# Attention with a relative bias and a mixture of adapters on one core: an earlier fetch of the last tokens, five staging buffers with a lead one pair longer, and edge factors ahead of gating on GpSimd

## The chip, the core and the metric

The kernel runs on one core of a Trainium2 chip. The core has TensorE (PE in the profile, its weight loads PEld), VectorE (DVE), ScalarE (ACT), GpSimd (POOL) and SyncE (SP), each with an instruction queue of its own that it works off in order. In this kernel nearly all DMAs are issued by SyncE. The metric is the time of one execution on the device, in microseconds.

## What is computed

```python
def _attn_ref(q, k, v, bias_table):             # q, k, v: (8, 8, 576, 64)
    scores = scale * np.matmul(q, k.transpose(0, 1, 3, 2))
    ...
    bias = bias_table[bucket]                   # bucket depends on |i - j| alone
    scores = scores + bias.transpose(2, 0, 1)[None, :, :, :]
    ...
    attn = np.exp(scores)
    attn = attn / (np.sum(attn, axis=-1, keepdims=True) + 1e-09)
    return np.matmul(attn, v).astype(np.float32)

def _moe_ref(x, w_gate, A, B):                  # x: (4608, 512), 8 experts, rank 16, two per token
    logits = x @ w_gate
    ...
            z = x[mask] @ A[e]
            delta[mask] += w[mask, k, None] * (z @ B[e])
    return (x + delta).astype(np.float32)
```

The output of the attention of all heads, side by side, is the x of the adapters. The weights w are the softmax over the two largest logits of a token.

## The kernel before

The work is cut into 32 pairs: pair u is batch b = u // 4 and the two heads 2 hp and 2 hp + 1 with hp = u % 4. The main loop (L747) runs over the pairs, and all instructions stand in an order written out by hand. The 576 tokens of a batch are 512 main tokens, in four chunks of keys, and 64 last tokens, called the tail. The tails of q, k and v are fetched once for a batch, for all its heads.

Loading: `load` (L103) issues on SyncE the main tokens of q (one DMA of 256 KB) and of k and v (two of 128 KB each) of one pair into a staging pool with four buffers for each of q, k, v (L70). `load_tail` (L118) issues three DMAs of 128 KB for a batch, for tails of q and k in one tile (qkt) and of v in another (vt), of which there are two each. Their rows in memory are 64 floats long. In pair u the loop issues q and k of pair u + 4 and v of pair u + 3 (L757 to L762), in pairs with hp = 0 ahead of them the tails of batch b + 1 (L753), in pair 2 the adapter weights (`weights_load`, L283), and in pair 1, between the two, the tails of batch 1. SyncE also issues the stores of the output (L617, L605) and, at some pairs, the DMAs that transpose x (`send_x`, L355).

Casting: GpSimd turns float32 into bfloat16. `prep(u)` (L722) casts q and k of pair u + 2 (L141) and v of pair u (L137), at the head of pair u from pair 4 on. `prep_tail` (L730) casts the tail of batch b + 1: that of q and k (qkb, L149) in the pair with hp = 1 and that of v (vb, L153) in the pair with hp = 2. The adapter weights are cast by VectorE at the end of pair 3 (`weights_cast`, L290, its first cast L291) and turned by TensorE in pairs 4 and 5 (L300).

Scores: TensorE turns q and k of pair u + 1 in pair u (L317), VectorE copies the result (qkT, L321). `keys` makes the scores of one chunk with the bias (L376, L381), `keys_exp` their exponential on ScalarE (pk, L387), four of 128x1024 a pair. `edges` (L409), at the end of pair u for pair u + 1, makes the scores between the main tokens and the tail and their exponential (pt, L424). The bias of pt is not added before the exponential but multiplied in afterwards: `edge_bias` (L426), two multiplications on GpSimd with the factors ELC and ET (L430, L432), in the pair to which pt belongs.

Values: in pair u + 1 TensorE multiplies the probabilities of pair u with v: `values_b` and `values_a`, the chunks by L440, the tail's keys by L450, which reads pt, and the tail's rows by L464. VectorE divides by the sums (L508, L521, L528) and writes x.

Adapters: x is turned by TensorE (L348) or by a transposing DMA (L357), multiplied with A and the gate weights (L541), and VectorE finds the two largest logits, their sum, the argument of the tanh and the mask (L555, L560, L562, L565). The gating itself is `moe_w` (L568): a tanh on ScalarE, whose program place is behind the second exponential of a pair, and three instructions on GpSimd (g L574, gate L576, zt L578). zt is turned by TensorE (L586) one to three pairs later, ahead of that pair's L440 of `values_b`, multiplied with B (L593), and VectorE adds x (ot, L596). On GpSimd the gating of a pair (`run(gate1...)`, L768) stands behind that pair's casts and ahead of its `edge_bias`; in the last pair alone `edge_bias` stands ahead of it (L766).

Of the kernel before, what the change touches and what calls it, by code (L numbers as in the profile page):

```python
# [26 lines left out]
def _ap(t, offset, dims):  # L27

    return bass.AP(tensor=t.tensor, offset=t.offset + offset, ap=[list(t.ap[0])] + dims)
# [8 lines left out]
def kernel(  # L38
# [12 lines left out]
    B, H, S, D = q.shape  # L51
# [5 lines left out]
    HP = H // 2  # L57
# [9 lines left out]
    ctx.enter_context(tc.manual_schedule())  # L67

    cp = ctx.enter_context(tc.tile_pool(name="const", bufs=1))
    stg = ctx.enter_context(tc.tile_pool(name="staging", bufs=4))  # L70
    stt = ctx.enter_context(tc.tile_pool(name="tailstaging", bufs=2))
    qkp = ctx.enter_context(tc.tile_pool(name="qk", bufs=2))
    ep = ctx.enter_context(tc.tile_pool(name="probs", bufs=2))
# [17 lines left out]
    NU = len(units)  # L91
# [11 lines left out]
    def load(u, names="qkv", eng=nc.sync):  # L103
        b, hp = units[u]
        for nm in names:
            src = {"q": q, "k": k, "v": v}[nm]
            t = stg.tile([128, 2, 4 * D], FP32, name=f"{nm}s", tag=f"{nm}s")
            heads = src[b, 2 * hp:2 * hp + 2, :SM, :]
            if nm != "q":
                for h in range(2):  # L110
                    eng.dma_start(out=t[:, h, :].rearrange("p (g x) -> p g x", g=2),
                                      in_=heads[h].rearrange("(g p c) d -> p g (c d)", g=2, c=2))
            else:
                eng.dma_start(out=t, in_=heads.rearrange("h (p c) d -> p h (c d)", c=4))
            stage[(u, nm)] = t


    def load_tail(b, names="qkv", g0=0, g1=HP, eng=nc.sync):  # L118
        for nm in names:
            src = {"q": q, "k": k, "v": v}[nm][b, :, SM:, :]  # L120
            if nm == "v":
                t = stt.tile([64, H, D], FP32, name="vt", tag="vt")
                eng.dma_start(out=t, in_=src.rearrange("g p d -> p g d"))
            else:
                if (b, "qk") not in tstage:
                    tstage[(b, "qk")] = stt.tile([128, H, D], FP32, name="qkt", tag="qkt")
                t = tstage[(b, "qk")]
                o = 0 if nm == "q" else 64
                eng.dma_start(out=t[o:o + 64, 2 * g0:2 * g1],
                              in_=src[2 * g0:2 * g1].rearrange("g p d -> p g d"))  # L130
            tstage[(b, nm)] = t
# [151 lines left out]
    def weights_load():  # L283
        nc.sync.dma_start(out=A4f.rearrange("p e c r -> p e (c r)"),
                          in_=moe_A.rearrange("e (p c) r -> p e (c r)", c=4))
        nc.sync.dma_start(out=G4f.rearrange("p c e -> p (c e)"),
                          in_=moe_w_gate.rearrange("(p c) e -> p (c e)", c=4))
        nc.sync.dma_start(out=Bf, in_=moe_B.rearrange("e r d -> (e r) d"))
# [97 lines left out]
    def keys_exp(u, c):  # L386
        nc.scalar.activation(probs[u][0][c], scs.pop(c), ACT.Exp, scale=scale)  # L387
# [38 lines left out]
    def edge_bias(u, eng=nc.gpsimd):  # L426
        b, hp = units[u]
        pt = probs[u][1]
        tl = _ap(pt, 64 + 256 + 96, [[SM, 2], [128, 2], [1, 32]])
        nc.gpsimd.tensor_tensor(tl, tl, _ap(ELC, hp * 64, [[SM, 2], [32, 2], [1, 32]]), op=ALU.mult)  # L430
        te = _ap(pt[64:], 64 + 128, [[SM, 2], [1, 128]])
        eng.tensor_tensor(te, te, ET[64:, :, hp, :], op=ALU.mult)  # L432
# [289 lines left out]
    def prep(u):  # L722
        b, hp = units[u]
        if u + 2 < NU:
            for nm in ("q", "k") if u > 2 else ("k",):
                cast(u + 2, nm, nc.gpsimd)
        if u:
            cast(u, "v", nc.gpsimd)
# [18 lines left out]
    for u in range(NU):  # L747
        b, hp = units[u]
        if hp == 0 and b:
            moe(b - 1, u)  # L750
        if u > 3:
            prep(u)
        if hp == 0 and 0 < b < B - 1:  # L753
            load_tail(b + 1)
        if u == 2:
            weights_load()
        if u + 4 < NU:  # L757
            load(u + 4, "qk")
        if u == 1:
            load_tail(1)  # L760
        if u + 3 < NU:
            load(u + 3, "v")  # L762
        for c in KO[:2]:
            keys(u, c)
            keys_exp(u, c)
        if u == NU - 1:  # L766
            edge_bias(u)
        run(gate1.pop(u, []))  # L768
        if u:
            if u < NU - 1:  # L770
                edge_bias(u)
            if u < 4:
                prep(u)
            if u == 6:
                nc.gpsimd.tensor_scalar(Bc, Bf, 0.5, None, op0=ALU.mult)
            prep_tail(u)
        zb, ta, xa = zs.pop(u, []), zts.pop(u, []), xas.pop(u, [])
        if u:
            pa = pva.pop(u - 2, None)
            oa = 256 if xa or hp == 0 else (ER + E) * (len(zb) > 1)  # L780
            ia = (XO - oa) // 64

            def bank_b():
                pv = values_b(u - 1)
                zl = pv[:, 260:260 + ER + E]
                for gr, t in zb[:1]:
                    moe_z(gr, t, zl, False)
                o = 260 + (ER + E) * bool(zb)
                for i, (gr, t) in enumerate(ta[ia:]):
                    moe_t(gr, t, pv, o + i * 64)  # L790
                return pv, zl

            if pa is not None:
                for gr, t in xa:
                    turn_x(gr, t, pa)
                values_x(u - 2, pa)
                for i, (gr, t) in enumerate(ta[:ia]):
                    moe_t(gr, t, pa, oa + 64 * i)
                za = pa[:, :ER + E]
                for gr, t in zb[1:]:  # L800
                    moe_z(gr, t, za, True)
                for gr, t in xa:
                    copy_x(gr, t)
                for gr, t in ta[:ia]:
                    moe_tc(gr, t)
                normalise_x(u - 2, pa)
                for gr, t in zb[1:]:
                    moe_zc(gr, t, za)
            pv, zl = bank_b()
            for gr, t in ta[ia:]:  # L810
                moe_tc(gr, t)
            normalise_b(u - 1)
            for gr, t in zb[:1]:
                moe_zc(gr, t, zl)
            if u < 16:
                run(dl2.pop(u, []))
            if hp == 0:
                corners(pa[:, :256], b)
            run(send.pop(u, []))
        else:  # L820
            t = Turn()
            turn_tail(t, 0, 2)
            copy_tail(t, 0, 2)
            corners(mp.tile([128, 256], FP32, name="cps", tag="mm"), 0)
        keys(u, KO[2])
        keys_exp(u, KO[2])
        run(dl2.pop(u, []))
        if 0 < u < NU - 1:
            t = Turn()
            turn_qk(t, u + 1)  # L830
            if hp == HP - 1:
                turn_tail(t, b + 1)
            xt = xts.pop(u, [])
            x0 = 16 - 4 * len(xt)
            for i, (gr, c) in enumerate(xt):
                for j in range(4):
                    t.block(x0 + 4 * i + j, gr.x[c][:, j * 128:j * 128 + 128])
            copy_qk(t, u + 1)
            if xt:
                gr, c = xt[0]  # L840
                gr.open()
                t.copy(gr.xT[:, c:c + len(xt)], x0, 4 * len(xt))
            if hp == HP - 1:
                copy_tail(t, b + 1)
        keys(u, KO[3])
        keys_exp(u, KO[3])
        run(dls.pop(u, []))
        if u in (4, 5):
            weights_turn(u - 4)
        if u == 0:  # L850
            factors_l()
            factors_t()
            corners_bias(0)
            edge_bias(0)
            prep(0)
        else:
            if hp == 0:
                corners_bias(b)
            values_a(u - 1)
            if u == NU - 1:  # L860
                values_x(u - 1, pva[u - 1])
            normalise_a(u - 1)
            if u == NU - 1:
                normalise_x(u - 1, pva[u - 1])
            for gr, i in zb:
                at(gates, gr.late or u, moe_g, gr, i)
            run(gates.pop(u, []))
            run(sendx.pop(u, []))
        if u < 3:
            cast(u + 2, "q", nc.vector)  # L870
        if u == 3:
            weights_cast()
        if u == NU - 1:
            break
        if u:
            open_probs(u + 1)
            edges(u + 1)


        order = slots[-3:]  # L880
# [242 lines left out]
```

## Time and profile before

| | |
|---|---|
| median of three runs | 196.53 us (194.33, 196.53, 196.64) |
| the profiled execution | 195.78 us, its span 193.9 us |
| granted TensorE clock | 0.992 of full speed |
| VectorE, GpSimd busy | 136.2 us (70%), 138.7 us (72%) |
| moved by DMA | 41.77 MB, 215 GB/s in the mean |

The times of engines and instructions come from the one profiled execution, counted from the start of its span. A row of a timeline gives start, duration, engine, line of the kernel, operation and tiles, and in brackets how long the engine had been idle before it and what released it. A wait for several events is put down to the one that came last by the profile, which can be the wrong one. A row of the stretches gives, for a piece of the span, the busy time of PE, PEld, DVE, ACT and POOL with the number of instructions, the granted clock, the share of DMA and its GB/s.

### The profile page before, as it was taken

To read this page: it belongs to the slowest core of one execution; us is meant where nothing else is said; L and a number is where in the kernel's file an instruction comes from. 1 tells how busy PE (TensorE), PEld (TensorE's weight loads), DVE (VectorE), ACT (ScalarE), POOL (GpSimd) and SP (SyncE) were. 2 spreads that over 40 slices of the span, in tenths; PEclk is the share of its full clock that TensorE was granted. 3 is DMA by queue.
4 is the path that set the end of the run, shared out by engine and by line. 5 is a ranking of instruction groups with operands and counts; after the bars stand their busy time and mean duration, and the time that the engine had idled before them with its cause. 6 is when DMAs were issued, how large, how long until landed. Compare 5 with 4: busy or idle time off the path is not lost.

```text
span 193.9 us, 11323 instructions
## 1 busy us (share of the span) xinstructions
PE 167.9 (87%) x4833; PEld 121.3 (63%) x4834; DVE 136.2 (70%) x460; ACT 166.2 (86%) x206; POOL 138.7 (72%) x286
## 2 busy tenths in 40 slices
PE   0459798999999998999989999995899999999970
PEld 0335466777777776677766676673667676666840
DVE  4421466656758975899779778984779998888760
ACT  3159999999999999999989899995898899789680
POOL 5086945898996998589978857649898885876030
PEclk9999999999999999999999999999999999999996
DMA  5679797998868996889786887689879998855356
GB/s 149 183 163 253 234 239 193 269 225 216 246 177 219 173 273 213 215 211 261 247 218 175 215 247 181 180 255 237 247 222 256 238 185 254 269 187 146 112 229 205
DMA packets 72047, 41.77 MB, mean 215 GB/s; under 512 B 25773, under 2 KB 67253, under 8 KB 71997
## 3 DMA queue, kind: packets, MB, share of 16 engines
q1 hardware_dynamic: 71084, 40.58, 77.4%
q8 instruction: 37, 0.61, 1.5%
q10 hardware_dynamic: 912, 0.48, 1.0%
q14 instruction: 14, 0.11, 0.2%
HBM read 29.67 MB, written 9.47 MB: 202 GB/s over the span
## 4 chain that ended last, share of the span: by engine, by line
PE 53%; DVE 13%; DMA 9%; ACT 9%; POOL 5%; issue 5%; SPq 3%; ACTq 1%; POOLq 0%; DVEq 0%
PE sc L376 11%; PE pv L440 11%; ACT pk L387 7%; PE sc L381 6%; DMA qkt<-in_k_dram 5%; PE tp L317 4%; PE dl L593 4%; PE pv L464 4%; PE pv L450 3%; PE sc L417 3%; PE pv L541 3%; DMA Wt<-g_d 2%; DVE ot L596 2%; PE pv L348 2%; DMA ks<-in_k_dram 2%
## 5 line engine op out<-in xcount | busy, mean ns | idle before, releaser
L387 ACT ACTIVATE pk<-sc 128x1024 bf16<-128x1024 f32 x128 | 124.3, 1032 | 6.8 <-PE sc L381 6.4
L376 PE MATMUL sc<-qkT 64*64 64x512 bf16 x512 | 53.1, 394 | 2.4 <-issue 1.1
L381 PE MATMUL sc<-Wt,antw 64*64 64x384 bf16 (+1 forms) x512 | 44.5, 301 | 1.3 <-DMA Wt<-g_d 1.2
L440 PEld LDWEIGHTS <-pk 128*128 128x128 bf16 x1024 | 39.5, 98 | 7.8 <-issue 4.7
L440 PE MATMUL pv<-v,pk 128*128 128x65 bf16 x992 | 42.1, 194 | 1.7 <-POOL v L137 1.4
L424 ACT ACTIVATE pt<-sc 128x1024 bf16<-128x1024 f32 x32 | 32.8, 1025 | 10.1 <-PE sc L422 8.6
L321 DVE COPY qkT<-tp 128x1024 bf16<-128x1024 bf16 x32 | 22.1, 689 | 8.8 <-PE tp L317 7.7
L508 DVE TENSOR_TENSOR xn<-pv,rc 128x256 bf16<-128x256 f32 x56 | 23.8, 425 | 1.9
L141 POOL CAST kn<-ks 128x512 bf16<-128x512 f32 x30 | 18.4, 613 | 8.8 <-DMA ks<-in_k_dram 4.4
L376 PEld LDWEIGHTS <-qkT 64*64 64x64 bf16 x512 | 18.0, 107 | 9.7 <-issue 3.7
L432 POOL TENSOR_TENSOR pt<-pt,ET 64x256 bf16<-64x256 bf16 x32 | 21.4, 668 | 2.5
L141 POOL CAST qn<-qs 128x512 bf16<-128x512 f32 x27 | 16.5, 610 | 5.4 <-PE tp L317 3.5
L137 POOL CAST v<-vs 128x512 bf16<-128x512 f32 x32 | 20.0, 625 | 0.1
L381 PEld LDWEIGHTS <-antw 64*64 64x64 bf16 x512 | 17.9, 108 | 3.1 <-issue 2.6
L450 PE MATMUL pv<-vb,pt 128*128 128x130 bf16 x124 | 17.3, 220 | 2.4 <-POOL pt L430 2.4
L596 DVE TENSOR_TENSOR ot<-dl,xn 128x512 f32<-128x512 f32 x25 | 17.1, 685 | 0.4 <-PE dl L593 0.2
L317 PE MATMUL tp<-ident,qn 64*64 64x64 bf16 x512 | 11.7, 196 | 5.2 <-ACT qn L141 5.2
L317 PEld LDWEIGHTS <-qn 64*64 64x64 bf16 x512 | 10.7, 111 | 8.6 <-ACT qn L141 5.2
L430 POOL TENSOR_TENSOR pt<-pt,ELC 128x128 bf16<-128x128 bf16 x32 | 13.6, 426 | 1.1 <-ACT pt L424 0.6
L317 PE MATMUL tp<-ident,kn 64*64 64x64 bf16 x512 | 12.0, 197 | 2.0 <-issue 1.5
L464 PEld LDWEIGHTS <-pt 128*128 128x128 bf16 x256 | 10.5, 98 | 5.0 <-issue 5.0
L464 PE MATMUL pv<-v,pt 128*128 128x65 bf16 x248 | 13.2, 194 | 0.1
(144 smaller groups left out, 309.5 us busy)
## 6 DMA issues: line engine op xcount, KB each, us to landing
qs<-in_q_dram SPq DMA_DIRECT2D x32, 256.0 KB, 3.6
vs<-in_v_dram SPq DMA_DIRECT2D x64, 128.0 KB, 4.2
ks<-in_k_dram SPq DMA_DIRECT2D x62, 128.0 KB, 4.0
out_dram<-ot SPq DMA_DIRECT2D x25, 256.0 KB, 3.8
vt<-in_v_dram SPq DMA_DIRECT2D x8, 128.0 KB, 5.6
out_dram<-fot SPq DMA_DIRECT2D x4, 256.0 KB, 2.1
qkt<-in_q_dram SPq DMA_DIRECT2D x7, 128.0 KB, 5.6
qkt<-in_k_dram SPq DMA_DIRECT2D x7, 128.0 KB, 4.0
```

Source lines behind the costliest of these rows:

```text
L141: copy(t.rearrange("p c h d -> p h c d"), s)
L317: nc.tensor.transpose(self.ps[h * 64:h * 64 + 64, f, x * 64:x * 64 + 64], src[rows, h * 64:h * 64 + 64], ident[rows, rows])
L321: nc.vector.tensor_copy(_ap(dst, 0, [[64, 2], [128, n], [1, 64]]), self.ps[:, :, x * 64:(x + n) * 64].rearrange("p f (x t) -> p f x t", t=64))
L376: nc.tensor.matmul(sc[prt, h, :], lhsT=kT[rows, c * 128 + f * 64:c * 128 + f * 64 + 64], rhs=qT[rows, :], start=True, stop=False, skip_gro ...
L381: nc.tensor.matmul(_ap(sc[prt, h, :], p0, [[128, 4], [1, n]]), lhsT=turned_w(h), rhs=_ap(Wt[rows, hp, :], (1 - e) * GY + y0, [[GY, 4], [1, ...
L387: nc.scalar.activation(probs[u][0][c], scs.pop(c), ACT.Exp, scale=scale)
L424: nc.scalar.activation(probs[u][1][:, 64:], sc.rearrange("p h x -> p (h x)"), ACT.Exp, scale=scale)
L432: eng.tensor_tensor(te, te, ET[64:, :, hp, :], op=ALU.mult)
L440: nc.tensor.matmul(pv[:, o + h * W1:o + (h + 1) * W1], lhsT=pk[c][:, h, t * 128:(t + 1) * 128], rhs=vm[:, c, h, :], start=(first and h == ...
L450: nc.tensor.matmul(_ap(pv, o + h * W1, [[130, n], [1, W1]]), lhsT=pt[:, x0:x0 + 128], rhs=tvs[b % 2][:, t // 2:t // 2 + n, 2 * hp + h, :], ...
L464: nc.tensor.matmul(pv[:, o + h * W1:o + (h + 1) * W1], lhsT=src[:, x0:x0 + 128], rhs=rhs, start=(first and h == 0), stop=False, skip_group ...
L508: nc.vector.tensor_tensor(dst, _ap(pv, 0, [[2 * W1, 2], [W1, 2], [1, D]]), _ap(rc, i, [[2, 2], [1, 2], [0, D]]), op=ALU.mult)
```

## The change

Four things change in the text; no instruction is added or removed, only their order and the number of staging buffers.

- The staging pool has five buffers instead of four for each of q, k and v.
- The tails of batch b + 2 are issued in the pair of batch b with hp = 2, for batches 2 to 7, instead of those of batch b + 1 in the pair with hp = 0. Their casts stay where they are: a tail's q and k are now issued three pairs ahead of their cast, and v four, instead of one and two. The tails of batch 1 are issued in pair 1 as before.
- Up to pair 8, q and k are issued four pairs ahead and v three; from pair 8 on five and four, so that pair 8 issues two pairs of each.
- `edge_bias` stands ahead of the gating in every pair from pair 1 on, not in the last alone.

```diff
-    stg = ctx.enter_context(tc.tile_pool(name="staging", bufs=4))
+    stg = ctx.enter_context(tc.tile_pool(name="staging", bufs=5))
...
-        if hp == 0 and 0 < b < B - 1:
-            load_tail(b + 1)
+        if hp == HP - 2 and 1 < b + 2 < B:
+            load_tail(b + 2)
         if u == 2:
             weights_load()
-        if u + 4 < NU:
-            load(u + 4, "qk")
+        for n in (u + 4,) * (u < 9) + (u + 5,) * (u > 7):
+            if n < NU:
+                load(n, "qk")
         if u == 1:
             load_tail(1)
-        if u + 3 < NU:
-            load(u + 3, "v")
+        for n in (u + 3,) * (u < 9) + (u + 4,) * (u > 7):
+            if n < NU:
+                load(n, "v")
         for c in KO[:2]:
             keys(u, c)
             keys_exp(u, c)
-        if u == NU - 1:
+        if u:
             edge_bias(u)
         run(gate1.pop(u, []))
         if u:
-            if u < NU - 1:
-                edge_bias(u)
             if u < 4:
                 prep(u)
```

## The prediction

> **What bounds the kernel now.** I read the page first, then the busy time by stretches, the waits, and the timelines of the single engines around the places that the waits point to.
>
> ```profile
> PE 167.9 (87%) x4833; PEld 121.3 (63%) x4834; DVE 136.2 (70%) x460; ACT 166.2 (86%) x206; POOL 138.7 (72%) x286
> ```
>
> and by stretches:
>
> ```profile
> 45.00:98.00 53.00, 51.54 (x1571) 38.42 (x1571) 41.30 (x137) 51.62 (x62) 44.94 (x84) 1.00 0.84 223
> 130.00:141.00 11.00, 8.05 (x249) 5.99 (x245) 6.48 (x26) 8.06 (x12) 8.92 (x19) 1.00 0.92 246
> 98.00:176.00 78.00, 72.92 (x2137) 51.99 (x2122) 64.47 (x225) 69.64 (x86) 59.52 (x118) 1.00 0.83 222
> ```
>
> TensorE and ScalarE are busy 87% and 86% of the span, so the body can only be as short as the exponentials and the products, and what can be won is idle time of ScalarE. The stretches (busy time of PE, PEld, DVE, ACT, POOL in this order) say where it lies. From 45 to 98 us ScalarE idles 53.00 - 51.62 = 1.38 us, 2.6%. From 98 to 176 us it idles 78.00 - 69.64 = 8.36 us; at 2.6% it would be 2.03, so 6.33 us are in excess there, and 2.94 of the 8.36 lie in the 11 us from 130 on. That is the place to read.
>
> ```profile
> 122.44 0.69 SPq L129 DMA_DIRECT2D qkt<-in_q_dram  x1
> ...
> 125.45 0.63 SPq L114 DMA_DIRECT2D qs<-in_q_dram  x1
> 126.12 0.98 SPq L111 DMA_DIRECT2D ks<-in_k_dram  x2
> ```
>
> then GpSimd:
>
> ```profile
> 127.32 0.61 POOL L149 CAST qkb<-qkt 128x512 bf16<-128x512 f32 x1 [0.42 <-DMA qkt<-in_k_dram]
> 128.60 0.61 POOL L141 CAST qn<-qs 128x512 bf16<-128x512 f32 x1 [0.67 <-DMA qs<-in_q_dram]
> 130.89 0.61 POOL L141 CAST kn<-ks 128x512 bf16<-128x512 f32 x1 [1.68 <-PE pv L586]
> 131.45 0.62 POOL L137 CAST v<-vs 128x512 bf16<-128x512 f32 x1
> ...
> 132.63 0.62 POOL L578 TENSOR_TENSOR zt<-z,gate 128x256 bf16<-128x256 f32 x1
> 133.20 0.42 POOL L430 TENSOR_TENSOR pt<-pt,ELC 128x128 bf16<-128x128 bf16 x1
> ```
>
> then TensorE and ScalarE:
>
> ```profile
> 132.12 0.68 PE L440 MATMUL pv<-v,pk 128*128 128x65 bf16 x16 [1.35 <-POOL v L137]
> 133.68 0.29 PE L450 MATMUL pv<-vb,pt 128*128 128x130 bf16 x2 [0.89 <-POOL pt L430]
> ```
>
> ```profile
> 134.81 1.94 ACT L387 ACTIVATE pk<-sc 128x1024 bf16<-128x1024 f32 x2 [2.39 <-PE sc L381]
> ```
>
> Each row is start, duration, engine, line, and the idle time before it. SyncE issues the tail loads of the next batch at the head of pair 20 (122.44 to 125.45: 3.01 us), and only then q and k of pair 24, whose k is issued at 126.12. GpSimd casts exactly these in its pair 21 and 22: the tail after 0.42 us of idleness, q after 0.67, k after 1.68. The profile names L586 as the releaser of the last, but the k cast reads nothing that L586 makes and the k load went out only 4.77 us before it; I take it for the load. Behind it in GpSimd's queue stand the cast of v, the gating (zt) and only then the edge factor (pt); TensorE waits 1.35 us for v and 0.89 for pt, and ScalarE 2.39 for TensorE.
>
> **Part one: the longer lead.** From pair 8 on, q, k, v are issued one pair sooner, and the tails from the pair with hp = 2, ahead of where they were by two pairs. Buffers do not object: with five of them the load of pair n takes the buffer of pair n - 5, whose cast of q and k stands two pairs ahead of that issue, the same distance as with four buffers and the shorter lead. So the waits of GpSimd on loads go, from its pair 11 on, the first whose q and k went out early.
>
> ```profile
> POOL qkb L149 <- DMA qkt<-in_k_dram: 9.4, 4, 3.5
> POOL g L574 <- ACT th L572: 6.2, 6, 2.2
> ```
>
> ```profile
> 170.10 1.02 ACT L424 ACTIVATE pt<-sc 128x1024 bf16<-128x1024 f32 x1 [0.64 <-POOL g L574]
> ```
>
> Most of GpSimd's waiting is covered: it costs only where TensorE comes to wait for GpSimd. Of the 9.4 us on tails, all but the 0.42 above fall before 31 us in GpSimd's timeline, on the loads of batches 0 and 1, which the change leaves where they are: no gain. What I book is the stretch from 130 to 141: its idle time falls from 2.94 to the 2.6% of the quiet stretch, 0.29: minus 2.65 us. To it I add the one wait of ScalarE that is put down to GpSimd, minus 0.64. Gain 3.3 us; its bounds are 0 (VectorE is as late right behind) and the 6.33 us of the excess.
>
> The five extra issues at pair 8 (q, two of k, two of v, about 2.4 us at 0.49 each by the 126.12 row) delay on SyncE the two transposes of that pair, which are read two and three pairs later. I book nothing; uncovered it would be 2.4 us once.
>
> **Part two: what the moved tail pushes back.** The tails of batch 2 used to be issued at the head of pair 4; now they are issued at the head of pair 2, in front of the adapter weights and of q, k of pair 6.
>
> ```profile
> 28.79 1.56 SPq L284 DMA_DIRECT2D A4f<-in_moe_A_dram  x1
> ```
>
> ```profile
> 37.36 0.61 SPq L129 DMA_DIRECT2D qkt<-in_q_dram  x1
> ...
> 40.06 0.57 SPq L114 DMA_DIRECT2D qs<-in_q_dram  x1
> ```
>
> and of the DMA issues (KB, us to landing), VectorE, GpSimd and TensorE:
>
> ```profile
> A4f<-in_moe_A_dram SPq DMA_DIRECT2D x1, 256.0 KB, 4.1
> ```
>
> ```profile
> 33.59 0.56 DVE L291 CAST A<-A4f 128x512 bf16<-128x512 f32 x1
> ...
> 35.51 0.18 DVE L528 RECIPROCAL rc<-pv 128x4 f32<-128x4 f32 x1 [0.41 <-PE pv L450]
> ...
> 36.45 0.69 DVE L321 COPY qkT<-tp 128x1024 bf16<-128x1024 bf16 x1 [0.30 <-PE tp L317]
> ```
>
> ```profile
> 37.03 0.61 POOL L141 CAST kn<-ks 128x512 bf16<-128x512 f32 x1 [0.16 <-DMA ks<-in_k_dram]
> ```
>
> ```profile
> 39.80 0.68 PE L440 MATMUL pv<-v,pk 128*128 128x65 bf16 x16
> ```
>
> The three tail issues took SyncE 40.06 - 37.36 = 2.70 us. SyncE issues one load after the other there, so A4f goes out at 28.79 + 2.70 = 31.49 and, landing 4.1 us after its issue, is there at 35.6; VectorE reaches its cast at 33.59 and now stands 2.0 us. Queued behind it are the normalisation of pair 2's tail rows, which frees the bank for TensorE, and the copy of qkT for pair 5, which the next scores read. VectorE's idle 0.41 and 0.30 absorb 0.7 of it, so qkT comes 1.3 us late. ScalarE is the bound here and does not get that back: plus 1.3 us. The bounds are 0 (a landing that owes less to SyncE than I think) and 2.7 (nothing absorbed).
>
> The Trainium skill has a rule that would make this dearer: DMA: Bandwidth & Descriptors, Specifications, says that pieces under 512 B do not move at line rate, and a tail moves in rows of 64 floats, 256 B. By that page the 384 KB of tails would weigh like twice the bytes, an estimate of 3.5 us at the 223 GB/s of the stretch from 45 on, 2.1 us late after the same 0.7 and 0.7, and a sum 0.8 us higher. No row here separates rings from SyncE's issue, so it stays at the upper edge.
>
> GpSimd's k of pair 6 moves from 37.03 to 39.7 by the same 2.70, and the cast of v behind it from 37.6 to 40.3; TensorE reads that v at 39.80, which becomes 41.1 with the 1.3 above: covered by 0.8. From pair 4 on the tail issue that stood there is gone, and SyncE is level again; at pair 6 and 8 the same exchange repeats with nothing like A4f in it, and I book zero.
>
> **Part three: edge factors ahead of gating.** No instruction is added. The edge factors no longer stand behind a gating that waits for tanh, 6.2 us of idle GpSimd time in all, which is hidden now; zero by itself, but it is why pt of 133.20 would be earlier. In exchange zt comes later by the two edge multiplications.
>
> ```profile
> L432 POOL TENSOR_TENSOR pt<-pt,ET 64x256 bf16<-64x256 bf16 x32 | 21.4, 668 | 2.5
> ...
> L430 POOL TENSOR_TENSOR pt<-pt,ELC 128x128 bf16<-128x128 bf16 x32 | 13.6, 426 | 1.1 <-ACT pt L424 0.6
> ```
>
> and where one pair's zt meets its reader, with VectorE's sum of the two top logits (ns min/median/max):
>
> ```profile
> 125.13 0.62 POOL L578 TENSOR_TENSOR zt<-z,gate 128x256 bf16<-128x256 f32 x1
> ```
>
> ```profile
> 125.81 0.23 PE L586 MATMUL pv<-ident,zt 128*128 128x128 bf16 x1
> ```
>
> ```profile
> L560 DVE TENSOR_TENSOR sn<-top x17: 159/307/641, 58.4 to 175.9; 128x2 f32<-128x2 f32 x14, 128x1 f32<-128x1 f32 x3
> ```
>
> That is 0.668 + 0.426 = 1.09 us. At pair 21 there is no room for it as things stand: zt ends at 125.75 and TensorE turns it at 125.81. With GpSimd no longer held up by loads (above) it is ahead by more than that, so zero; without that cover it costs 1.09 us in each pair whose zt is read in the next.
>
> **The sum.** The profiled execution took 195.78 us, its span 193.9 and 1.88 around it. 195.78 - 2.65 - 0.64 + 1.3 = 193.8. The median of the three runs shown is 196.53, 0.75 above the profiled one, and the lowest 194.33; I leave the sum on the profiled time.
>
> **The rivals.** *The early cost does not bite and the lead is worth more:* A4f is not on time by SyncE's issue alone, and the excess from 98 on is largely late loads. For it speak GpSimd's k and q waits in that stretch, against it that VectorE is busy 64.47 of the 78 us there. No early cost, and half of what I did not book of the excess, (6.33 - 3.29) / 2 = 1.5: 195.78 - 3.29 - 1.5 = 191.0.
>
> *VectorE takes the place of the loads:* GpSimd without its waits runs against VectorE's gating more often. The sum of the two top logits (sn) took from 159 to 641 ns, median 307, for two elements a partition; if all seventeen took the longest, that is 17 x 0.334 = 5.7 us more on VectorE, enough to eat the 3.3. Left is the early cost: 195.78 + 1.3 = 197.1. The Trainium skill has the rule for this spread (SBUF — State Buffer, Who interferes with whom): an operation of VectorE with two SBUF inputs and one of GpSimd that reads SBUF lock each other out, whoever starts first keeps the port. By that rule the durations of sn are what remains of a GpSimd operation at that moment, and the trace's spread agrees with it.
>
> *Slower, zt on the path:* the gating is pushed behind the edge factors while GpSimd is still late. In ten pairs zt is read in the very next pair; in two of them (9 and 13) the wait for tanh has room for the edge work, in eight not. 8 x 1.09 = 8.7, plus the early 1.3, less the wait for pt of 0.89 that the new order does remove: 204.9. It decides from four such pairs on. Against it: the loads would have to be as late as now in spite of one pair more.
>
> That the change doesn't do what it says I give nothing: the issues move by the program's order, and SyncE issues in that order.
>
> **How the numbers follow.** Forecast 0.40 (its own range 192.3 to 195.4), better 0.33, VectorE 0.16, slower 0.11. 2% is 3.9 us, about what a measurement of this kernel can tell from no change: faster means under 191.9, slower over 199.7. So faster 0.33, same 0.56, slower 0.11. The range goes from 190.2, a fifth of the better case lying below it down to 195.78 - 6.33 = 189.4, to 198.0, the VectorE case with the 2.1 us of the rings; left out are the slower case and that fifth.
>
> **What would show it.** The cast of k (L141) without a wait on ks from pair 11 on; L440 and L450 without waits for GpSimd after 98 us; ScalarE's idle time from 98 on near 5 us instead of 8.36; VectorE's cast of A4f standing some 2 us on its load near 33.6, and ScalarE idle behind it; g (L574) no longer waiting for tanh. The prediction is wrong if that cast does not wait, if L586 comes to wait for zt, or if VectorE's waits fill the place of GpSimd's.

## The result, and the profile after

| | before | changed |
|---|---|---|
| median of 22 runs each | 196.30 us (193.37 to 197.73) | 198.79 us (195.67 to 204.01) |
| profiled execution, span | 195.78 us, 193.9 us | 197.79 us, 195.8 us |
| granted clock in it | 0.992 | 0.983 |

The changed kernel is slower: ratio 1.011, 95% interval 1.0062 to 1.0158. (A ratio is made of the undisturbed runs of both kernels, a median of all.) The forecast was 193.8: the change is under 2%, and it goes the other way.

The changed kernel by the same three stretches (busy PE, PEld, DVE, ACT, POOL, then clock, DMA share, GB/s):

```profile
45.00:98.00 53.00, 51.76 (x1556) 38.69 (x1555) 41.23 (x135) 51.54 (x63) 45.65 (x86) 1.00 0.86 226
130.00:141.00 11.00, 10.43 (x315) 7.85 (x312) 8.80 (x28) 10.79 (x15) 10.17 (x21) 1.00 0.83 232
98.00:176.00 78.00, 72.84 (x2099) 52.03 (x2097) 63.00 (x221) 68.65 (x85) 58.58 (x118) 0.98 0.85 214
```

From 130 to 141 us ScalarE now idles 0.21 us instead of 2.94: what was forecast to go is gone. But from 98 to 176 it idles 78.00 - 68.65 = 9.35 us, more than the 8.36 before. GpSimd's waits in the changed kernel (us in all, times, longest) also moved as forecast:

```profile
POOL kn L141 <- DMA ks<-in_k_dram: 2.2, 3, 0.9
POOL g L574 <- ACT th L572: 0.8, 1, 0.8
```

Before, the wait of g was 6.2 us, and that of the k cast:

```profile
POOL kn L141 <- DMA ks<-in_k_dram: 4.4, 6, 2.1
```

So the time was lost after the stretch that was won. ScalarE's L424 comes once a pair; numbered from 0, these are its starts 2, 12, 25 and 31 in the changed kernel:

```profile
23.95 1.02 ACT L424 ACTIVATE pt<-sc 128x1024 bf16<-128x1024 f32 x1
...
73.29 1.02 ACT L424 ACTIVATE pt<-sc 128x1024 bf16<-128x1024 f32 x1 [0.28 <-PE sc L422]
...
138.87 1.02 ACT L424 ACTIVATE pt<-sc 128x1024 bf16<-128x1024 f32 x1
...
177.20 1.02 ACT L424 ACTIVATE pt<-sc 128x1024 bf16<-128x1024 f32 x1 [0.29 <-PE sc L422]
```

and in the kernel before:

```profile
23.84 1.02 ACT L424 ACTIVATE pt<-sc 128x1024 bf16<-128x1024 f32 x1
...
72.72 1.02 ACT L424 ACTIVATE pt<-sc 128x1024 bf16<-128x1024 f32 x1 [0.19 <-PE sc L422]
...
142.60 1.02 ACT L424 ACTIVATE pt<-sc 128x1024 bf16<-128x1024 f32 x1
...
175.41 1.02 ACT L424 ACTIVATE pt<-sc 128x1024 bf16<-128x1024 f32 x1 [0.29 <-PE sc L422]
```

Up to start 12 the changed kernel takes 49.34 us against 48.88, up to 25 it takes 65.58 against 69.88, and from there to 31 it takes 38.33 against 32.81: 4.3 won in the middle, 5.5 given back behind it. What stands there, in TensorE's timeline of the changed kernel:

```profile
77.01 0.22 PE L317 MATMUL tp<-ident,kn 64*64 64x64 bf16 x2 [0.94 <-issue]
...
134.78 0.39 PE L464 MATMUL pv<-v,pt 128*128 128x65 bf16 x7 [0.47 <-issue]
...
144.70 0.39 PE L440 MATMUL pv<-v,pk 128*128 128x65 bf16 x7 [0.79 <-issue]
...
150.07 0.35 PE L381 MATMUL sc<-Wt,antw 64*64 64x384 bf16 x4 [0.75 <-issue]
...
155.17 0.26 PE L317 MATMUL tp<-ident,kn 64*64 64x64 bf16 x8 [0.38 <-issue]
...
161.92 0.20 PE L394 MATMUL pv<-tl 64*64 64x64 bf16 x1 [2.33 <-issue]
```

In the kernel before such waits come to 2.40 us at five places, the four shown here and 0.60 at 99.28:

```profile
76.25 0.22 PE L317 MATMUL tp<-ident,kn 64*64 64x64 bf16 x2 [0.76 <-issue]
...
81.35 0.31 PE L317 MATMUL tp<-ident,kn 64*64 64x64 bf16 x14 [0.31 <-issue]
...
117.47 0.29 PE L317 MATMUL tp<-ident,kn 64*64 64x64 bf16 x12 [0.41 <-issue]
...
164.28 0.41 PE L376 MATMUL sc<-qkT 64*64 64x512 bf16 x4 [0.32 <-issue]
```

"issue" means that the profile shows nothing that was waited for. The place says what it was: counted in the trace, each of the six in the changed kernel is the first instruction behind number 192 past a multiple of 256 in TensorE's own stream of 9,673, and the page has a DMA queue for instructions alone:

```profile
q8 instruction: 37, 0.61, 1.4%
```

37 packets (MB, share) for 9,673 instructions are 261 to a packet, 16 KB each. TensorE stands at the seams between these blocks. The packet of the block behind the 2.33 us began to move when TensorE had 19 instructions left; for the other blocks of this execution it was 91 to 248. The sixteen profiles of this document have 69 such waits (over 0.3 us, after 60 us): all 69 stand at that place in the count, and after 68 of them TensorE goes on 1.0 to 1.7 us behind the end of the block's packet. So these are waits for TensorE's own instructions. Short stretches around the longest show what followed:

```profile
152.00:155.00 3.00, 2.79 (x81) 2.11 (x73) 2.57 (x13) 3.00 (x5) 2.13 (x5) 1.00 1.55 304
...
158.00:161.00 3.00, 1.59 (x41) 1.37 (x40) 1.88 (x10) 2.32 (x4) 1.53 (x4) 1.00 1.04 229
161.00:164.00 3.00, 2.08 (x81) 1.52 (x80) 0.22 (x1) 1.40 (x2) 1.93 (x3) 0.66 0.91 281
164.00:167.00 3.00, 3.00 (x70) 1.91 (x63) 2.67 (x9) 1.77 (x3) 1.75 (x4) 0.77 0.59 204
```

The packets that start in the first of these stretches take 1.55 times its length on the 16 engines, those that start around the stand 1.04 times; TensorE stands, and then it runs at half clock for 3.41 us, which the clock of 0.66 and 0.77 in two stretches adds up to. That pair took 8.90 us, start 28 to 29 of L424, against 5.15 before.

### The profile page after: what moved, and what is told of

The parts are those of the page before. It is cut to its first block, busy times and chain, and to the rows that moved or that the text cites. A ratio compares the mean times of both kernels' runs of the same rounds, so it can differ in the third digit from the quotient of the medians.

```text
span 195.8 us, 11328 instructions
## 1 busy us (share of the span) xinstructions
PE 169.4 (87%) x4833; PEld 122.7 (63%) x4834; DVE 135.5 (69%) x460; ACT 166.2 (85%) x206; POOL 138.1 (71%) x286
## 2 busy tenths in 40 slices
DMA packets 72046, 41.77 MB, mean 213 GB/s; under 512 B 25772, under 2 KB 67252, under 8 KB 71996
## 4 chain that ended last, share of the span: by engine, by line
PE 66%; ACT 8%; DMA 6%; issue 6%; SPq 5%; DVE 5%; POOL 1%; ACTq 0%; DVEq 0%; POOLq 0%
PE sc L376 15%; PE pv L440 14%; PE sc L381 7%; ACT pk L387 7%; PE dl L593 5%; PE pv L464 5%; PE tp L317 5%; PE sc L417 3%; PE pv L541 3%; PE pv L450 3%; DMA G4f<-in_moe_w_gate_dram 2%; PE pv L348 2%; SPq L111 2%; PE sc L422 2%; DMA qs<-in_q_dram 2%
## 5 line engine op out<-in xcount | busy, mean ns | idle before, releaser
L376 PE MATMUL sc<-qkT 64*64 64x512 bf16 x512 | 54.2, 400 | 1.6 <-ACT pk L387 1.1
L381 PE MATMUL sc<-Wt,antw 64*64 64x384 bf16 (+1 forms) x512 | 45.2, 305 | 2.6 <-DMA Wt<-g_d 1.8
L440 PEld LDWEIGHTS <-pk 128*128 128x128 bf16 x1024 | 39.8, 98 | 6.7 <-issue 3.3
L440 PE MATMUL pv<-v,pk 128*128 128x65 bf16 x992 | 42.8, 194 | 0.9 <-issue 0.8
L424 ACT ACTIVATE pt<-sc 128x1024 bf16<-128x1024 f32 x32 | 32.8, 1026 | 10.4 <-PE sc L422 9.1
L376 PEld LDWEIGHTS <-qkT 64*64 64x64 bf16 x512 | 18.7, 108 | 12.5 <-issue 6.2
L450 PE MATMUL pv<-vb,pt 128*128 128x130 bf16 x124 | 17.2, 220 | 0.8 <-POOL pt L430 0.8
L404 POOL TENSOR_TENSOR pc<-pcx,ELC 64x256 bf16<-64x256 bf16 x16 | 10.6, 665 | 6.5 <-ACT pcx L398 3.5
```

The costliest lines, as they stand in the source:

```text
L376: nc.tensor.matmul(sc[prt, h, :], lhsT=kT[rows, c * 128 + f * 64:c * 128 + f * 64 + 64], rhs=qT[rows, :], start=True, stop=False, skip_gro ...
L381: nc.tensor.matmul(_ap(sc[prt, h, :], p0, [[128, 4], [1, n]]), lhsT=turned_w(h), rhs=_ap(Wt[rows, hp, :], (1 - e) * GY + y0, [[GY, 4], [1, ...
L424: nc.scalar.activation(probs[u][1][:, 64:], sc.rearrange("p h x -> p (h x)"), ACT.Exp, scale=scale)
L440: nc.tensor.matmul(pv[:, o + h * W1:o + (h + 1) * W1], lhsT=pk[c][:, h, t * 128:(t + 1) * 128], rhs=vm[:, c, h, :], start=(first and h == ...
L450: nc.tensor.matmul(_ap(pv, o + h * W1, [[130, n], [1, W1]]), lhsT=pt[:, x0:x0 + 128], rhs=tvs[b % 2][:, t // 2:t // 2 + n, 2 * hp + h, :], ...
```

## The experiments

The table at the end of this section gives the stretches between starts of L424 and, as "standing", the sum of all waits of TensorE over 0.3 us that are put down to "issue" after 60 us. Medians of the kernel before on the same chip stand beside each group; the groups ran on three chips, and a profile is of one execution.

**Each part alone.** On this chip the kernel before had 198.09 us (17 runs). Edge factors ahead of gating, alone:

```diff
-        if u == NU - 1:
+        if u:
             edge_bias(u)
         run(gate1.pop(u, []))
         if u:
-            if u < NU - 1:
-                edge_bias(u)
```

> Before, with only the edge factors put ahead of the gating. Theory A: the time that the change loses is TensorE standing without anything that the profile shows it waiting for, because the fetches of its own instructions (16 KB each on the DMA engines) come late among denser loads; the order on GpSimd changes no transfer, so this kernel takes the time of before within 0.5 us, or up to 1 us less where pt was late. Rival B: zt, now 1.09 us later, is late at the turn by TensorE in the pair after the gating; then this kernel alone carries the loss, 2 us or more over before, with waits of L586 on zt.

197.57 us, ratio 1.0102 (1.0055 to 1.0149): by the medians 0.5 us under the kernel before, by the ratio 1% above it. Theory A's 0.5 us fits the medians and not the ratio. Rival B falls by its mechanism: TensorE waited for zt three times, 0.37 us at most. What it does show is standing at places where the kernel before had none:

```profile
140.52 0.41 PE L376 MATMUL sc<-qkT 64*64 64x512 bf16 x3 [1.20 <-issue]
...
160.92 0.19 PE L394 MATMUL pv<-tl 64*64 64x64 bf16 x1 [1.47 <-issue]
```

That is against theory A too: no load is issued earlier here, and yet this profile stands 4.30 us.

The early tails alone:

```diff
-        if hp == 0 and 0 < b < B - 1:
-            load_tail(b + 1)
+        if hp == HP - 2 and 1 < b + 2 < B:
+            load_tail(b + 2)
```

> Before, with only the tails issued two pairs sooner. Theory A: the loads are as dense as before save that the tail of batch 2 stands in front of the adapter weights; 0.5 to 1 us more than before at pair 4, and some of it won back where the tail was late at GpSimd: within 1 us of before. Rival C: the early tails cost it all, through A4f and the loads behind the tail at pairs 2 and 6: 2 us or more over before, all of it lost by 60 us.

202.01 us (6 runs, no ratio), 3.9 us up by the medians, more than theory A allows. The load of A4f is late as forecast for the change, and more so (VectorE, then TensorE behind it):

```profile
36.01 0.43 DVE L291 CAST A<-A4f 128x512 bf16<-128x512 f32 x1 [2.61 <-DMA A4f<-in_moe_A_dram]
```

```profile
36.97 0.22 PE L394 MATMUL pv<-tl 64*64 64x64 bf16 x3 [1.96 <-DVE xe L521]
80.63 0.22 PE L317 MATMUL tp<-ident,kn 64*64 64x64 bf16 x2 [2.40 <-issue]
...
162.30 0.26 PE L317 MATMUL tp<-ident,kn 64*64 64x64 bf16 x8 [2.10 <-issue]
```

Each of these three was followed by half clock. Start 4 to 5 took 8.18 us against 5.16. That is theory C's mechanism; that it would be over by 60 us is wrong, for the seams at 80 and 162 cost as much again.

The buffers and the longer lead alone, the tails where they were:

```diff
-    stg = ctx.enter_context(tc.tile_pool(name="staging", bufs=4))
+    stg = ctx.enter_context(tc.tile_pool(name="staging", bufs=5))
...
-        if u + 4 < NU:
-            load(u + 4, "qk")
+        for n in (u + 4,) * (u < 9) + (u + 5,) * (u > 7):
+            if n < NU:
+                load(n, "qk")
...
```

> Before, with only five staging buffers and the lead one pair longer for q, k, v from pair 8 on. Theory A: loads go out earlier and denser, the instruction fetches of TensorE come late: 2 us or more over before and a wide spread like that of the changed kernel, with stalls of TensorE of over 0.7 us put down to issue. Rivals B and C: the loads are then only earlier, the stall of 2.4 us near 132 us goes, and the time is 2 to 3 us under before.

200.66 us, ratio 1.0285 (1.0201 to 1.0369): the size that theory A gave, but in part by another way. With q, k, v a pair sooner and the tail not, the tail is the late load (GpSimd, then TensorE):

```profile
128.75 0.61 POOL L149 CAST qkb<-qkt 128x512 bf16<-128x512 f32 x1 [5.66 <-DMA qkt<-in_k_dram]
```

```profile
131.09 0.88 PE L440 MATMUL pv<-v,pk 128*128 128x65 bf16 x16 [2.30 <-POOL v L137]
```

Start 23 to 24 took 10.51 us. So in this profile the longer lead lacks the earlier tail, and the earlier tail alone collided with the adapter weights.

**Is it the early cost, the bytes, or the place of the buffers?** The kernel before had 197.20 us (23 runs) on this chip. The changed kernel with its tails issued last in their pair:

```diff
-        if hp == HP - 2 and 1 < b + 2 < B:
-            load_tail(b + 2)
         if u == 2:
             weights_load()
...
                 load(n, "v")
+        if hp == HP - 2 and 1 < b + 2 < B:
+            load_tail(b + 2)
```

> The changed kernel, with the tails of batch b + 2 still issued in the pair with hp = 2, but behind that pair's weights, q, k and v loads and no longer ahead of them. Theory C (the early cost of the tail in front of the adapter weights is what the change loses): the wait of VectorE on A4f near 34 us and TensorE's wait for xe behind it go, and the kernel comes out 1.5 to 3 us below the changed one, level with the kernel before. Theory A (the loss is TensorE standing for its own instructions after 140 us, and the half clock behind the longest of these stands): the early 0.5 us alone is won, the standing after 140 us stays, and the kernel lies 0 to 1 us below the changed one, that is 0.5 to 2.5 us above the kernel before.

200.34 us, ratio 1.0209 (1.01 to 1.0319). Start 4 to 5 falls to 5.31 us, so the early cost is gone, and the kernel is no faster for it: 3.1 us above the kernel before, where the changed kernel has a ratio of 1.011. Theory C falls, and theory A's 0.5 to 2.5 us is passed too. Standing is 5.66 us, and a transposing DMA is late on top:

```profile
157.63 0.41 PE L541 MATMUL pv<-AW,xT 128*128 128x136 bf16 x4 [2.31 <-DMA xT<-xn]
```

Both kernels without the stores of two batches:

```diff
-        gr.store, gr.left = store, len(gr.x)
+        gr.store, gr.left = store if b not in (3, 4) else (lambda ot, t=0: None), len(gr.x)
```

> The kernel before, without the stores of the output of batches 3 and 4, which leaves these rows of the output unwritten and takes some 2.3 MB of writes out of the pairs 22 to 28, and nothing else. It is the base for the next run. Theory A (TensorE's instruction fetches share the DMA engines with loads and stores): its standing without a releaser between 130 and 170 us, 1.0 us in all in the kernel before, goes to under 0.5, and the time falls by 0 to 1 us. Rival B2 (the long lead costs through GpSimd and VectorE, and DMA traffic plays no part): the time stays within 0.5 us of the kernel before.

> The changed kernel without the same stores (the output rows of batches 3 and 4 stay unwritten). Theory A: the standing of TensorE without a releaser after 140 us, 4.7 us in the profile of the changed kernel with 2.33 before the q, k rows of L394 at 161.9, falls under 1.5 us, no half clock follows, and the kernel is 1 to 3 us faster than the kernel before without these stores. Rival B2: it stays 1.5 to 3 us slower than the kernel before without these stores, as the changed kernel stands to the kernel before now.

193.62 us (ratio 0.9851, 0.9746 to 0.9955) and 194.97 us (0.992, 0.9827 to 1.0013). The kernel before gains 3.6 us where theory A had 0 to 1, and B2 none; its standing between 130 and 170 us is gone, as A said, but the 1.0 us that the expectation counts there is too little for the gain. In the changed one no standing over 0.3 us is left after 140 us and no half clock in the body, as A said; that it would then overtake the other it did not, it lies 1.35 us above. That is so near B2's 1.5 to 3 us that these times don't exclude it.

The kernel before with `bufs=5` alone:

> The kernel before with five staging buffers in the place of four and nothing else: the addresses of what is allocated behind them move, and no instruction does. Theory A and theory C: within 0.5 us of the kernel before. Rival D (where buffers lie in SBUF decides 1 us or more, and so part of what the change shows has nothing to do with its loads): 1 us or more to either side.

197.78 us, ratio 1.0037 (0.9972 to 1.0102). Rival D falls. As no instruction moves in it, it serves below as another profile of the old order.

**The same kernels again, and thin stores.** The kernel before had 197.71 us (12 runs) on this chip.

> The kernel before, unchanged, for a second profiled execution of it. Theory E (the waits of TensorE on GpSimd near 132 us, the 2.65 us that the forecast booked as gain, belong to one execution and not to the kernel): pair 23 to 24, exponential to exponential of L424, takes 4.9 to 5.4 us in this profile as it does with five buffers alone, not the 7.47 of the first, and standing of TensorE without a releaser appears at other pairs than in the first profile, 2 to 4 us in all after 60 us. Rival F (the late load is in the program's order): pair 23 to 24 takes 6.8 to 7.6 us again, with TensorE waiting 1 us or more for v.

> The changed kernel, unchanged, for a second profiled execution. Theory A: TensorE's standing without a releaser comes to 3 us or more after 60 us, at the same instruction numbers (192 past a multiple of 256) but with other sizes, so that the 8.90 us of pair 28 to 29 need not recur; pair 23 to 24 stays at 4.9 to 5.2. Rival G (the standing at L394 of pair 28 is fixed by what the new order puts there): 2 us or more at that place again and a half clock behind it.

Second profile of the kernel before (198.06 us), TensorE:

```profile
137.35 0.68 PE L440 MATMUL pv<-v,pk 128*128 128x65 bf16 x16 [0.42 <-POOL v L137]
138.67 0.29 PE L450 MATMUL pv<-vb,pt 128*128 128x130 bf16 x2 [0.65 <-POOL pt L430]
```

Theory E holds in the main: start 23 to 24 took 5.33 us, not 7.47; the wait for GpSimd is there a pair later and half as long. Standing, at 1.50 us, fell short of its 2, and two of the three stands are at seams of the first profile. With five buffers alone TensorE waits 0.26 us there and no more. Second profile of the changed kernel (208.52 us, longer than any other run of it), TensorE:

```profile
144.33 0.41 PE L376 MATMUL sc<-qkT 64*64 64x512 bf16 x3 [1.35 <-issue]
...
148.00 0.23 PE L586 MATMUL pv<-ident,zt 128*128 128x128 bf16 x1 [1.20 <-POOL zt L578]
...
158.92 0.23 PE L586 MATMUL pv<-ident,zt 128*128 128x128 bf16 x1 [1.08 <-POOL zt L578]
162.67 0.63 PE L541 MATMUL pv<-AW,xT 128*128 128x136 bf16 x4 [3.51 <-DMA xT<-xn]
...
171.58 0.19 PE L394 MATMUL pv<-tl 64*64 64x64 bf16 x1 [0.48 <-issue]
```

Rival G falls: at the L394 of the 2.33 us there is 0.48, and the worst pair is another one, 12.04 us (start 27 to 28), by a transposing DMA that comes 3.51 us late. Theory A's standing came, 5.51 us, but it doesn't hold that wait. Transposes are late in the old order too: TensorE waits 0.89 us for one in the second profile of the kernel before, and 0.93 with five buffers alone. And one load is late in spite of the longer lead (GpSimd):

```profile
144.34 0.61 POOL L141 CAST kn<-ks 128x512 bf16<-128x512 f32 x1 [3.56 <-DMA ks<-in_k_dram]
```

Behind this cast stand the edge factors and the gating, and zt is what TensorE waits for at 148.00.

Then both kernels with their body stores cut to 8 of 128 partitions, so that SyncE's queue is as it was:

```diff
-                                  [:, c:c + 2 * n - 1:2, :], in_=ot)
+                                  [:8, c:c + 2 * n - 1:2, :], in_=ot[:8])
```

> The kernel before with the output stores of the body cut to 8 of their 128 partitions: as many stores at the same places of SyncE's queue with the same waits, but a sixteenth of their bytes, some 4 MB less; the other rows of the output stay unwritten. Unlike the runs that leave stores out, SyncE's order and waits are as they were. Theory A (bytes in flight delay the instruction fetches): 2 to 4 us faster than the kernel before, and under 1 us of standing without a releaser after 60 us. Rival H (what helped there was SyncE's freed queue, not the bytes): within 1 us of the kernel before.

> The changed kernel with the same cut of its body stores to 8 of 128 partitions (the other rows of the output stay unwritten). Theory A: the loss of the change goes with the bytes, so it lies within 0.7 us of the kernel before with the same cut, or below it. Rival B2: 1.5 us or more above that kernel. Rival H: within 1 us of the changed kernel itself.

191.81 us (ratio 0.9678, 0.9587 to 0.9769) and 192.13 us (0.9766, 0.9695 to 0.9837). The pages have 34.90 MB moved instead of 41.77, a cut of 6.9 MB and not of the 4 that the expectation names. Rival H falls. The two medians are 0.3 us apart, as theory A had it; but the runs of the kernel before go from 189.28 to 193.77 with one of 227.82, those of the changed one from 191.30 to 194.48, and by the ratios the changed kernel is 0.9%, 1.7 us, behind, with intervals that overlap. So the times alone do not decide between A and rival B2. The profiles say more. The late stretch, the kernel before and then the changed one with thin stores:

```profile
98.00:176.00 78.00, 76.28 (x2214) 54.83 (x2206) 68.57 (x235) 73.23 (x91) 61.51 (x123) 1.00 0.71 164
```

```profile
98.00:176.00 78.00, 77.21 (x2247) 55.54 (x2240) 68.95 (x237) 74.45 (x93) 61.94 (x124) 1.00 0.67 160
```

ScalarE idles 4.77 us in the one and 3.55 in the other, where with all stores it idles 8.36 and 9.35. So 3.6 us come free by the bytes alone, without the change. The change adds 1.2 us here, the way that was forecast, and loses 2.36 up to start 12 (51.16 against 48.80). The late loss is absent in this pair of profiles, which B2, for which the bytes play no part, does not explain.

**Where does the late loss come from?** The kernel before had 198.18 us (23 runs) on this chip. Three runs: the lead back to the old one at pair 20, then also batch 2's tail back in pair 4, and the changed kernel as their base:

```diff
-        for n in (u + 4,) * (u < 9) + (u + 5,) * (u > 7):
+        for n in (u + 4,) * (u < 9 or u > 20) + (u + 5,) * (7 < u < 20):
...
-        if hp == HP - 2 and 1 < b + 2 < B:
+        if hp == HP - 2 and 2 < b + 2 < B:
             load_tail(b + 2)
+        if u == HP:
+            load_tail(2)
```

The first hunk, and the same one for v, is the first run; both hunks are the second.

> The changed kernel, whose lead goes back to the old one at pair 20: that pair issues no q, k, v, and from pair 21 on they go out four and three pairs ahead as before the change; buffers, early tails and edge factors stay. Theory I (the loss after pair 25 comes from the long lead, whose loads run into the stores and transposes of the last pairs): pair 25 to 31, exponential to exponential of L424, falls from 38.3 us to 33 to 35, the gain up to pair 25 stays, and the kernel lies 2 us or more below the changed one. Theory J (the loss comes with any schedule here, as an accident of when stores, transposes and instruction fetches meet; the order only shifts where): 25 to 31 stays between 33 and 38 without a pattern, and the time within 1.5 us of the changed kernel.

> The kernel with the lead ended at pair 20, and the tail of batch 2 back at the head of pair 4, behind the adapter weights; the other tails stay early. By both theories VectorE's wait on A4f near 35 us goes, and pair 4 to 5 falls from 5.89 to 5.2 us: 0.5 to 1 us below the kernel with the lead ended. By theory I it is the order that beats both: 1 to 3 us below the kernel before. By theory J it is level with the kernel before, within 1.5 us.

> The changed kernel, unchanged, on the chip of the two runs before it, so that they can be set against it, and for a third profiled execution. Theory I: pair 25 to 31 takes 37 us or more, as in the two profiles there are (38.3 and 44.2). Theory J: it may come out anywhere from 33 us on.

199.70 us (ratio to the kernel before 1.0003, 0.992 to 1.0085), 200.00 us (1.0204, 1.0103 to 1.0304) and 202.16 us (1.0098, 0.9988 to 1.0208). The first lies 2.5 us below the changed kernel, as theory I said and theory J did not, but its last stretch took 36.51 us and not 33 to 35; the second, whose start 4 to 5 fell to 5.23 us as both theories said, and which should have beaten both kernels, is slower than before, with start 25 to 31 at 37.65 us. The third profile of the changed kernel has 35.95 us there, below theory I's 37. Theory I falls as a cause of the late loss by itself. Theory J fares no better on the second, which lies 1.8 us above the kernel before, where it allowed 1.5. The third profile of the changed kernel, TensorE:

```profile
78.65 0.22 PE L317 MATMUL tp<-ident,kn 64*64 64x64 bf16 x2 [1.49 <-issue]
...
133.54 0.22 PE L440 MATMUL pv<-v,pk 128*128 128x65 bf16 x2 [1.75 <-issue]
139.19 0.39 PE L464 MATMUL pv<-v,pt 128*128 128x65 bf16 x7 [1.62 <-issue]
...
163.59 0.19 PE L394 MATMUL pv<-tl 64*64 64x64 bf16 x1 [0.41 <-issue]
```

The same seams again (all at 192 past a multiple of 256), with other sizes: here the middle paid. All profiles side by side, in us:

| kernel (profiles) | start 2 to 12 | 12 to 25 | 25 to 31 | standing |
|---|---|---|---|---|
| before | 48.88 | 69.88 | 32.81 | 2.40 |
| before, second | 49.51 | 68.32 | 34.67 | 1.50 |
| before, five buffers | 49.28 | 66.36 | 34.89 | 1.60 |
| changed | 49.34 | 65.58 | 38.33 | 5.66 |
| changed, second | 52.77 | 66.48 | 44.16 | 5.51 |
| changed, third | 50.34 | 68.85 | 35.95 | 5.95 |
| edge factors alone | 48.53 | 67.04 | 36.61 | 4.30 |
| tails alone | 52.25 | 68.87 | 38.28 | 7.48 |
| lead and buffers alone | 48.68 | 70.63 | 36.98 | 2.99 |
| changed, tails behind | 48.66 | 68.78 | 36.23 | 5.66 |
| changed, lead ended | 50.56 | 67.39 | 36.51 | 4.15 |
| the same, tail 2 in pair 4 | 49.40 | 66.22 | 37.65 | 3.77 |
| before, two batches not stored | 49.00 | 68.23 | 33.27 | 3.07 |
| changed, two batches not stored | 49.14 | 64.88 | 34.02 | 1.48 |
| before, thin stores | 48.80 | 65.26 | 33.35 | 1.35 |
| changed, thin stores | 51.16 | 64.25 | 32.32 | 0.70 |

Three profiles of the old order (with five buffers alone among them) stand 1.5 to 2.4 us at the seams, three of the new one 5.5 to 6.0, and with thin stores it is 1.4 and 0.7. Standing isn't lost time one for one: without the stores of two batches the kernel before stands 3.07 us and is still 3.6 us faster.

## Why the prediction was wrong

By the medians of three profiles each (the old order with four buffers twice and with five once), the change costs 1.06 us from start 2 to 12 (50.34 against 49.28), wins 1.84 from 12 to 25 (66.48 against 68.32) and loses 3.66 from 25 to 31 (38.33 against 34.67): 2.9 us in all, against 2.49 between the medians of the two kernels. The forecast had +1.3, -3.3 and nothing. Only in the last stretch do the three and the three not overlap (32.81 to 34.89 against 35.95 to 44.16); the first two numbers are sizes from few executions.

**The sum** is the step that failed: "195.78 - 2.65 - 0.64 + 1.3 = 193.8" has no term for TensorE's waits for its own instructions, nor for a transposing DMA that lands late; both stand at nothing in it. The timeline of the kernel before showed the first, 2.40 us at five places, and the forecast left it as it was. Standing at the seams went from 1.60 to 5.66 us (the same medians), 4.1 us that the forecast left out. In the first profile 4.25 us of it lie between starts 25 and 31, and behind them half clock for 3.41 us, which costs 1.7 by estimate; together about the 5.5 us given back. In the second profile the transposing DMA adds 3.51. None of the rivals held it either: they asked which engine waits for which load, and none asked about the DMAs that no line of the kernel issues.

**"What I book is the stretch from 130 to 141"** was right in mechanism (no wait over 0.3 us of L440 or L450 for GpSimd after 98 us in any of the three profiles of the changed kernel; but the casts of k still wait for loads behind pair 11, up to 0.9, 3.56 and 0.9 us in the three) and too large. The 2.65 us were read from one execution, whose middle, 69.88 us, was the longest of the three; the second has 1.1 us of these waits at another pair and 0.27 at this one, five buffers alone 0.26. 1.84 us by the medians is what it was worth with the -0.64 in it. That last wait, ScalarE's at 170.10, is gone in the changed kernel, but the second profile of the kernel before hasn't it either.

**Part two, the early cost,** was right in place, kind and nearly in size: start 4 to 5 went from 5.16 to 5.89 us (medians), 0.7 for the 1.3 forecast. In the changed kernel:

```profile
34.80 0.43 DVE L291 CAST A<-A4f 128x512 bf16<-128x512 f32 x1 [1.27 <-DMA A4f<-in_moe_A_dram]
```

It stood 1.27 instead of 2.0 us, and 1.70 and 0.55 in the other two profiles. The dearer price by the Trainium skill (DMA: Bandwidth & Descriptors, Specifications), with its rule on pieces under 512 B, put the tails at an estimated 3.5 us and so this stand at 2.8 (3.5 less 0.7); none of these three shows that, though the tails alone came to 2.61. Taking this cost away (tails behind) didn't make the kernel faster.

**Part three** booked zero with a price of 1.09 us a pair where the cover is gone. It was zero in the first and third profile of the changed kernel; in the second TensorE waited 1.20 and 1.08 us for zt, the first of them behind the k load that was 3.56 us late, which is the lack of cover that the forecast named. The price was near, the number of pairs 0 to 2, not the 8 of that rival.

**The five extra issues** at pair 8, booked at zero, can't be told from the scatter: the lead alone takes 48.68 us up to start 12, the kernel before 48.88 to 49.51.

**VectorE takes the place of the loads** would have given 197.1, the nearest to the measured time, but not by its mechanism: VectorE was busy 135.5 us in the changed kernel against 136.2, and the sum of the top logits had medians of 221, 216 and 198 ns in its three profiles against 307, 191 and 191 in the old order, so it took no longer.

**The half clock** was in no term. Every run lists its mean clock: 0.984 in the mean of 22 runs of the changed kernel, and of 12 more on another chip, 0.989 in the mean of 75 runs of the kernel before. Half clock for t lowers that mean by t / 2 in some 196 us, so 0.005 is 2.0 us of half clock more per execution, which can cost 1.0 us: of the loss a part, not most of it. It is argued from the means, not measured by itself.

**What stays open:** that TensorE waits for its own instructions, and more in the changed kernel, is what the profiles show. That the bytes of the stores have to be in flight for the late loss fits the two pairs of runs with fewer bytes, but their times are too scattered to show it. Which loads meet the instruction fetches, and why the edge factors alone, which issue no load earlier, stand more than the old order, is open: ending the lead early and moving the tails changed sizes, and no run singled out one transfer. None of the versions with all stores has a ratio below 1 to the kernel before.

## What to carry to other kernels

Where the DMA engines are as busy as here (a share of 0.83 to 0.85 from 98 us on), don't take an earlier load as free: put into the sum a term for the DMAs that no line issues, the engine's own instructions above all, and look for "issue" in the chain and for waits at a fixed distance in the instruction count. Before a single wait is booked as a gain, see whether a second profile of the same kernel has it: here it had moved by a pair and halved. And when an edit takes away just the wait that it was meant to, and the time doesn't follow, tabulate the same event pair by pair in both traces: that shows at once where it was given back.

## What the runs showed of the hardware

- TensorE's instructions come in blocks of 256, and it can stand at the seams: up to 2.4 us at a time, 7.5 us in all after 60 us in the worst execution (tails alone). The Trainium skill (Runtime: NRT & Kernel Launch, Instruction fetch mechanics) calls the crossing of such a block mostly hidden. The runs with thin stores come near to that, with 0.7 and 1.4 us after 60 us; at the changed kernel's DMA share of 0.85, with 5.5 to 6.0, the trace does not agree.
- A single stand can be enough to halve the clock for 3.41 us, or for 6.83. Of the twelve stands of TensorE of 1.70 us or more between 20 and 185 us, in all the profiles and whatever was waited for, eight went with it (1.70, 1.87, 1.96, 2.10, 2.30, 2.33, 2.40 and 3.51 us) and four did not (1.75, 1.82, 1.83 and 2.31). The Trainium skill (TensorE: Matmul & The Clock Gate, Why this matters for your kernels) asks for no gaps over about 3 us; here 1.70 was too much once. The second profile of the changed kernel, behind its 3.51 us:

```profile
161.00:164.00 3.00, 1.33 (x21) 1.34 (x22) 0.63 (x4) 0.00 (x0) 2.69 (x7) 0.51 1.03 267
164.00:167.00 3.00, 3.00 (x75) 1.92 (x73) 1.55 (x5) 1.02 (x1) 1.27 (x3) 0.50 1.20 243
```

- One kernel's executions differ in which of these stands they meet, as the three profiles of the changed one show, and in time: 195.67 to 204.01 us in 22 runs. With thin stores its six runs lay between 191.30 and 194.48.
